# Transposing the rows' maxima: TensorE's transpose against VectorE's 32 by 32 blocks

## The chip, the cores and the metric

The kernel runs on one core of one Trainium2 chip. A core has TensorE (PE in the profile, with its weight loads as PEld), VectorE (DVE), ScalarE (ACT), GpSimd (POOL) and SyncE (SP), which here only issues DMAs. The metric is the device time of one execution in microseconds, lower is better. Three executions of the kernel before took 850.92, 851.16 and 852.25 us; the median is 851.16 us.

## The reference

The input x has 2048 rows of 640 numbers. It is normalized, xn = layernorm(x), and goes through two branches whose results are multiplied:

```python
xn = _layernorm(x, axis=-1)
s = _A_ref(xn, A_wqkv, A_wo)                         # attention: 32 heads of 20, window of 256 keys
g = _silu(_B_ref(xn, B_w1, B_b1, B_w2, B_b2))        # MLP 640 -> 1536 -> 640, squared relu
return x + s * g
```

In the attention, `scores = q k^T * 20 ** -0.5`, a query sees itself and the 255 keys before it, and a softmax over these keys weighs the values. Everything is float32. The softmax subtracts the largest score of each row before it takes the exponential; how that maximum gets to where it is needed is what the change is about.

## The kernel before, in words

Products are made of split operands: a float32 number is written as a high part that TensorE takes at full speed and a remainder, and three products stand for one.

**First stage** (lines 134 to 406). x is loaded, normalized, transposed and split; the values v and the first columns of q and k are made. q and k go to HBM in split form.

**Second stage, the long one** (lines 1222 to 1267). The 32 heads are worked on as 16 pairs, each pair in 16 steps of 128 queries: 256 steps, and 11 more for what lags behind. The two heads of a pair lie in the two halves of the 128 partitions, so TensorE runs two lanes side by side, lane 0 on partitions 0 to 63 and lane 1 on 64 to 127. A step s does this for its pair p and tile q:

- `scores` (L479): the scores of 128 queries against up to 384 keys, one product in each lane, into the tiles sps (two banks, tag "s").
- `maxima` (L487): VectorE adds the mask and takes each row's maximum, two instructions and two reads of the accumulator, into a column of mt. mt has 128 partitions (the queries) and a column for each head and each of four steps. There are two such tiles, used in turn.
- `scores_t` (L519), nine steps later (LAG): the same scores again, transposed, with keys on the partitions and queries along the free axis. The operands have two rows more: the queries' tile qs carries minus the maximum (high part and remainder) and the keys' tile ks carries ones, so the product comes out with the maximum subtracted.
- `exps` (L525 to L528): ScalarE takes the exponential out of the one pair tile stps, GpSimd cuts off what is masked.
- `values` (L547), once in four steps, two steps later again: probabilities times values.

Every four steps the columns of mt must become rows of qs. That is `max_rows` (L489 to L505), called in the step after the fourth (s % 4 == 0, L1250). TensorE transposes mt with an identity, 64 by 64 in each lane (L494), into an unused part of that step's stps. ScalarE copies eight rows out with the sign turned (L500, tile row), copies them again as high part (L501, tile mrow), GpSimd makes the remainder (L502), and two DMAs write them into qs (L504).

**What fills the time between.** All engines' orders are written out by hand (`manual_schedule`): what the program emits first, an engine does first. A generator, `filler`, hands out the remaining matrix products (the rest of q and k as qkps, the MLP's two layers as hps and yps, all L469) half a product per lane at a time. A planner keeps one clock per lane; each emitted product adds a fixed cost from a table (`COST`, L42: 0.067 for 128 columns, 0.12 for 256, 0.147 for 320). In each step `fill` emits filler until lane 0's clock reaches the step's share, `pace` times the step's number. `pace` (L1200) is the sum of the filler and of the scores and values, without the transposes of the maxima, divided by the steps. The transposes add COST[128] = 0.067 to each lane (`both`, L495). A filler product needs one of three PSUM banks, which comes free when VectorE (L888 for qkps, L996 for yps) or ScalarE (L961 for hps) has read it out: the eviction.

**Third stage, the output** (`out_filler`, L1150). When the filler is used up, the attention's result, loaded back from HBM (ob, L1107, and the sums' inverses, L1108), is scaled by VectorE (L1123), split (L1124, L1127) and multiplied by wo (wops, L607), and the result is multiplied by silu of the MLP, added to x and stored. It may begin while the last steps still run: the filler goes over into it.

Of the kernel before, what the change touches and what calls it, by code (L numbers as in the profile page):

```python
# [29 lines left out]
HP = P // 2  # L30
HALF = D // 2
# [22 lines left out]
def f32(ap):  # L54
    return ap.bitcast(F32)
# [3 lines left out]
def attn_mlp_kernel(ctx: ExitStack, tc, x, wqkv, wo, w1, b1, w2, b2, out):  # L59
# [38 lines left out]
    mts = [const.tile([P, HP], F32, name=f"mt{j}") for j in range(2)]  # L98
# [22 lines left out]
    def ones_rows(i):  # L121
        for h in range(2):
            nc.sync.dma_start(f32(ks[i])[h * HP + KR:h * HP + KR + 2].rearrange("a (c n) -> a c n", n=P), ones.unsqueeze(1).to_broadcast([2, S // P, P]))

# [9 lines left out]
    with tc.tile_pool(name="ph1v", bufs=2) as p1v, tc.tile_pool(name="ph1", bufs=2) as p1, tc.tile_pool(name="ph1x", bufs=4) as p1b, tc.tile_pool(name="ph1w", bufs=1) as p1w, tc.tile_pool(name="ph1t", bufs=2, space=PSUM) as p1t:  # L134
# [129 lines left out]
        with tc.manual_schedule(engines={E_.PE, E_.Activation, E_.DVE, E_.Pool, E_.SP}):  # L264
# [99 lines left out]
            for b in range(NB):  # L364
# [8 lines left out]
                if b == 0:  # L373
# [8 lines left out]
                    def loads1():  # L382
                        load_x(2)
                        spill_x(0)
                        nc.sync.dma_start(b1t, b1.rearrange("(c p) -> p c", p=P))
                        nc.sync.dma_start(b2t, b2.partition_broadcast(P))
                        ones_rows(0)
                        raws.extend(load_w(group_src(1, w), KC) for w in "qk")
# [100 lines left out]
    def max_rows(p, g, tps):  # L489
        i = p % 2  # L490

        def one(j):
            r = slice(j * HP, (j + 1) * HP)
            nc.tensor.transpose(tps[:HP, j, 3 * P:3 * P + HP], mts[g % 2][r, :], ident[r, r])  # L494
        both(lambda: one(0), lambda: one(1), COST[P])  # L495

        def rest():
            row = at2.tile([8, P], F32, tag="row", bufs=1, name="row")
            mrow = at2.tile([8, 2, P], F32R, tag="mrow", bufs=1, name="mrow")
            nc.scalar.activation(row.rearrange("m (j n) -> m j n", j=2), tps[:8, :, 3 * P:3 * P + HP], AF.Copy, scale=-1.0)  # L500
            nc.scalar.activation(mrow[:, 0, :], row, AF.Copy)  # L501
            nc.gpsimd.tensor_sub(mrow[:, 1, :], row, f32(mrow[:, 0, :]))  # L502
# [6 lines left out]
    def pair_tile():  # L509
        return ptp.tile([P, 2, BT], F32, tag="st", name="stps")  # L510
# [703 lines left out]
    with tc.manual_schedule(engines={E_.PE, E_.Activation, E_.DVE, E_.Pool, E_.SP}):  # L1214
        load_v(0)
        nc.vector.memset(ot, 0.0)
        loads = []
# [4 lines left out]
        for s in range(steps):  # L1222
# [8 lines left out]
            if a:  # L1231
# [3 lines left out]
                if s == 2:  # L1235
                    ones_rows(1)
# [8 lines left out]
            rows = None  # L1245
# [53 lines left out]
```

## Time and profile before

| | before |
|---|---|
| median of three executions | 851.16 us (850.92 to 852.25) |
| span of the profiled execution, first to last instruction | 849.5 us |
| TensorE's mean granted clock in it | 0.999 |
| TensorE busy / VectorE / ScalarE / GpSimd | 841.8 / 457.9 / 420.9 / 330.4 us |
| the long stage, first to last L479 | 116.7 to 739.4 us |
| products of the output, L607 | 774.2 to 845 us |

The profiled execution has no time of its own beside its span; its span of 849.5 us is 1.7 us less than the median. In rows of groups the columns are line, engine, operation, tiles and shapes and count, then busy us and mean ns of one, then idle time of the engine just before them with what ended it. In rows of time the first number is the start, the second the duration, both in us. In rows by windows each engine's busy time stands with the number of its instructions, then the granted clock, the share of time that the 16 DMA engines were busy, and GB/s. "PE busy" counts a time as busy when either lane works.

### The profile page before, as it was taken

What the parts mean: (1) busy time and instruction counts of PE and PEld (TensorE: products, weight loads), DVE (VectorE), ACT (ScalarE), POOL (GpSimd) and SP (SyncE); (2) the same over time, 40 slices, a digit from 0 to 9 for tenths busy, and PEclk for the clock granted to TensorE, in tenths of its full rate; (3) what the DMA queues carried; (4) which work ended last, traced back from release to release, by engine and by line L of the source; (5) the groups of instructions that cost most, each with busy time, mean ns of one, the idle gap of its engine ahead of it and who ended that gap; (6) DMA issues with size and microseconds to landing.
All of it is one profiled execution on the core that took longest, in us unless ns stands there. A gap on an engine that the chain in (4) does not pass through costs nothing.

```text
span 849.5 us, 25542 instructions
## 1 busy us (share of the span) xinstructions
PE 841.8 (99%) x10160; PEld 784.3 (92%) x10160; DVE 457.9 (54%) x1370; ACT 420.9 (50%) x792; POOL 330.4 (39%) x652
## 2 busy tenths in 40 slices
PE   9999999999999999999999999999999999999997
PEld 8999999888888999999999999999999999999997
DVE  7653126665567645455445466755455455436753
ACT  5232114545556763664653664853763754763321
POOL 6010002434334553553552553643553543542442
PEclk9999999999999999999999999999999999999999
DMA  7997587868979565337248245576456355467993
GB/s 248 316 403 286 176 207 260 268 215 266 309 246 288 152 196 151 93 116 200 79 151 219 86 126 151 141 224 188 111 163 199 109 166 190 129 155 212 291 233 118
DMA packets 94398, 166.42 MB, mean 196 GB/s; under 512 B 10952, under 2 KB 43848, under 8 KB 93256
## 3 DMA queue, kind: packets, MB, share of 16 engines
q1 hardware_dynamic: 94120, 164.64, 63.9%
q8 instruction: 80, 1.31, 0.7%
q14 instruction: 38, 0.31, 0.1%
q10 hardware_dynamic: 160, 0.16, 0.1%
HBM read 93.66 MB, written 70.52 MB: 193 GB/s over the span
## 4 chain that ended last, share of the span: by engine, by line
PE 97%; DVE 1%; DMA 1%; issue 0%; ACT 0%; SPq 0%; DVEq 0%
PE yps L469 21%; PE hps L469 21%; PE qkps L469 14%; PE ops L547 10%; PE wops L607 8%; PE vps L229 8%; PE stps L519 5%; PE sps L479 4%; PE qkps L206 3%; PE tps L173 1%; DMA qs<-q_d 0%; DMA xt<-in_A_x_dram 0%; PE tps L302 0%; PE stps L494 0%; PE warm_ps L316 0%
## 5 line engine op out<-in xcount | busy, mean ns | idle before, releaser
L487 DVE CUSTOM_DVE_ANT_0 junk<-sps,mask 128x384 bf16<-128x384 f32 (+2 forms) x512 | 272.6, 532 | 257.7 <-PE hps L469 73.4
L525 ACT ACTIVATE p<-stps 128x768 f32<-128x768 f32 (+2 forms) x256 | 197.4, 771 | 257.2 <-PE stps L519 209.8
L526 POOL TENSOR_SCALAR_AFFINE_SELECT p<-p 128x256 f32<-128x256 f32 x256 | 110.1, 430 | 322.3 <-ACT p L525 317.0
L469 PE MATMUL yps<-w,hh 64*128 64x320 f32 x1536 | 228.3, 310 | 0.8 <-DVE ysb L996 0.7
L469 PE MATMUL hps<-xb,w 64*128 64x256 f32 (+1 forms) x2100 | 218.6, 305 | 0.0
L469 PEld LDWEIGHTS hps<-xb,w 64*128 64x128 f32 x2100 | 199.2, 187 | 6.2 <-issue 5.1
L469 PEld LDWEIGHTS yps<-w,hh 64*128 64x128 f32 x1536 | 181.9, 185 | 5.9 <-issue 3.4
L469 PE MATMUL yps<-w,hl 64*128 64x320 f32 x768 | 174.1, 309 | 0.0
L479 PE MATMUL sps<-ks,qs 60*128 60x384 f32 (+2 forms) x512 | 142.5, 340 | 0.2 <-DVE mt L487 0.2
L519 PE MATMUL stps<-qs,ks 62*128 62x384 f32 (+2 forms) x512 | 136.0, 330 | 0.1
L469 PEld LDWEIGHTS yps<-w,hl 64*128 64x128 f32 x768 | 113.7, 185 | 1.7 <-issue 1.7
L469 PE MATMUL qkps<-xT,wgkh 64*128 64x512 f32 x320 | 100.4, 395 | 0.0
L469 PE MATMUL qkps<-xT,wgqh 64*128 64x512 f32 x320 | 97.8, 392 | 0.0
L528 POOL TENSOR_SCALAR_AFFINE_SELECT p<-p 128x256 f32<-128x256 f32 x224 | 93.6, 418 | 0.0
L547 PE MATMUL ops<-p,vp 128*21 128x128 f32 (+1 forms) x2112 | 92.8, 313 | 0.0
L519 PEld LDWEIGHTS stps<-qs,ks 62*128 62x128 f32 x512 | 88.2, 187 | 1.3 <-issue 0.4
L479 PEld LDWEIGHTS sps<-ks,qs 60*128 60x128 f32 x512 | 86.2, 185 | 2.3 <-DVE mt L487 0.8
L547 PEld LDWEIGHTS ops<-p,vp 128*21 128x21 f32 x2112 | 65.2, 100 | 23.6 <-issue 11.6
L229 PE MATMUL vps<-wv,xT 128*128 128x320 f32 x480 | 71.5, 308 | 0.0
L229 PEld LDWEIGHTS vps<-wv,xT 128*128 128x128 f32 x480 | 70.5, 188 | 0.1
L966 POOL TENSOR_TENSOR hl<-sq,hh 128x512 fp32r<-128x512 f32 x48 | 62.2, 1297 | 18.9 <-ACT sq L965 18.8
L607 PE MATMUL wops<-wo,oT 128*128 128x320 f32 x384 | 61.6, 309 | 0.0
(104 smaller groups left out, 1165.0 us busy)
## 6 DMA issues: line engine op xcount, KB each, us to landing
ks<-k_d SPq DMA_DIRECT2D x64, 240.0 KB
qs<-q_d SPq DMA_DIRECT2D x64, 240.0 KB
xb<-xs SPq DMA_DIRECT2D x60, 256.0 KB
xs<-xT SPq DMA_DIRECT2D x8, 1280.0 KB
k_d<-shm SPq DMA_DIRECT2D x19, 512.0 KB
q_d<-shm SPq DMA_DIRECT2D x19, 512.0 KB
y<-ysb SPq DMA_DIRECT2D x28, 320.0 KB
o<-osb SPq DMA_DIRECT2D x64, 128.0 KB
```

What stands on the lines that cost most here:

```text
L206: nc.tensor.matmul(ps, wt[:, c, :], xT[part][b][:, c * BT + t0:c * BT + t0 + n], start=m == 1, stop=m == 3 * KC)
L229: nc.tensor.matmul(ps, xT[xp][b][:, c * BT + t * P: c * BT + (t + 1) * P], wv[wp][:, c, nh * HALF:(nh + 1) * HALF], start=first and m == 0 ...
L469: return nc.tensor.matmul(out, a[r], b_[r], skip_group_check=True, **kw)
L479: nc.tensor.matmul(ss[hh][:, :nk], qs[i][o, q * P:(q + 1) * P], ks[i][o, k0 * P:k0 * P + nk], start=True, stop=True)
L487: nc.vector.tensor_tensor_reduce(out=junk[:, :nk], in0=ss[hh][:, :nk], in1=mask[:, 3 * P - nk:], scale=1.0, scalar=-3.0e38, op0=ALU.add, o ...
L519: nc.tensor.matmul(tps[:, hh, :n], ks[i][o, kb * P:(kb + 1) * P], qs[i][o, kb * P:kb * P + n], start=True, stop=True)
L525: nc.scalar.activation(p32[:, :, :n], tps[:, :, :n], AF.Exp, scale=SCALE)
L526: nc.gpsimd.affine_select(p32[:, :, 0:P], p32[:, :, 0:P], pattern=[[0, 2], [1, P]], compare_op=ALU.is_ge, fill=0.0, base=0, channel_multip ...
L528: nc.gpsimd.affine_select(p32[:, :, 2 * P:], p32[:, :, 2 * P:], pattern=[[0, 2], [-1, P]], compare_op=ALU.is_gt, fill=0.0, base=0, channel ...
L547: nc.tensor.matmul(ot[r0:r0 + VW, c0:c0 + len(part), :], vps[p][:, kb // 4, kb % 4, hh, :], pt[:, hh, :].rearrange("p (t n) -> p t n", n=P ...
L607: nc.tensor.matmul(ps, a, b_, start=j == 0, stop=j == n - 1)
L966: nc.gpsimd.tensor_sub(hh[1][:, :BT], sq, f32(hh[0]))
```

## The change

- The four steps' maxima are no longer transposed by TensorE. VectorE does it with four instructions, each a transpose of a block of 32 by 32 of mt into a strip of row, which is now a tile in SBUF of 32 rows. They are emitted right after the fourth step's maxima (s % 4 == 3) and not in the next step; the rest of `max_rows` still runs in the next step, after the exponentials.
- The transposes no longer add their 0.067 to the planner's clocks, and no longer write into stps.
- ScalarE's copy with the turned sign (L500) is gone. The rows of keys hold minus one instead of one, and qs gets the maxima with their own sign.
- mt has 32 columns instead of 64.

```diff
-    ones = const.tile([2, P], F32, name="ones")
-    nc.gpsimd.memset(ones, 1.0)
+    minus = const.tile([2, P], F32, name="minus")
+    nc.gpsimd.memset(minus, -1.0)
...
-    def max_rows(p, g, tps):
+    def max_rows(p, g):
         i = p % 2
-
-        def one(j):
-            r = slice(j * HP, (j + 1) * HP)
-            nc.tensor.transpose(tps[:HP, j, 3 * P:3 * P + HP], mts[g % 2][r, :], ident[r, r])
-        both(lambda: one(0), lambda: one(1), COST[P])
+        row = at2.tile([SQ, P], F32, tag="row", bufs=1, name="row")
+        for r in range(0, P, SQ):
+            nc.vector.transpose(row[:, r:r + SQ], mts[g % 2][r:r + SQ, :])
 
         def rest():
-            row = at2.tile([8, P], F32, tag="row", bufs=1, name="row")
             mrow = at2.tile([8, 2, P], F32R, tag="mrow", bufs=1, name="mrow")
-            nc.scalar.activation(row.rearrange("m (j n) -> m j n", j=2), tps[:8, :, 3 * P:3 * P + HP], AF.Copy, scale=-1.0)
-            nc.scalar.activation(mrow[:, 0, :], row, AF.Copy)
-            nc.gpsimd.tensor_sub(mrow[:, 1, :], row, f32(mrow[:, 0, :]))
+            nc.scalar.activation(mrow[:, 0, :], row[:8], AF.Copy)
+            nc.gpsimd.tensor_sub(mrow[:, 1, :], row[:8], f32(mrow[:, 0, :]))
...
-            rows = None
+            rows, made = made, None
...
-            if s % 4 == 0 and 0 < s <= NP * NT:
-                rows = max_rows((s - 1) // NT, (s - 1) % NT // 4, stp[0] if b else pair_tile())
             if a:
                 maxima(*a, *sc)
+                if a[1] % 4 == 3:
+                    made = max_rows(p, q // 4)
```

Where instructions move is seen in the engines' orders. VectorE in the changed program, around one group of four steps (junk and mt are the maxima, here L488; L993 is the eviction that was L996):

```order
L488 ISA junk,mt_100<-sps,mask 128x384
L488 ISA mt_100 128x1
L494 STREAM_TRANSPOSE row<-mt_100 32x32 x4
L993 TENSOR_TENSOR ysb<-yps,b2t 128x320
L488 ISA junk,mt_101<-sps,mask 128x384
```

The four transposes stand between the last maxima of a group and whatever followed them; here it is the eviction of a filler bank, as directly behind 14 of the 64 groups.

TensorE before, in a step with s % 4 == 0 (sps and stps are the scores and the transposed scores, yps is filler):

```order
L479 MATMUL sps<-ks_117,qs_116 128x128 x2
L519 MATMUL stps<-qs_1350,ks_1351 128x384 x2
L494 MATMUL stps<-ident,mt_101 64x64 x2
L469 MATMUL yps<-w_0_0_3886,hl 128x320 x2
L469 MATMUL yps<-w_0_0_3886,hh 128x320 x2
```

In the changed program (its L516 makes the transposed scores, its L470 the filler) the same step has the filler directly behind the transposed scores:

```order
L480 MATMUL sps<-ks_117,qs_116 128x128 x2
L516 MATMUL stps<-qs_1350,ks_1351 128x384 x2
L470 MATMUL yps<-w_0_2_4007,hh 128x320
L470 MATMUL yps<-w_0_0_3785,hh 128x320
L470 MATMUL yps<-w_0_0_3785,hl 128x320
```

The pair of transposes is gone, and since the planner's clocks lack its cost, filler moves up. Where that ends is seen on TensorE at the end of the attention. Before, the last values (L547) are followed by filler, 52 half products of it, and only then by the output:

```order
L547 MATMUL ops<-p_13921,vp_12681 21x256 x2
L547 MATMUL ops<-p_13921,vp_12681 21x128 x2
L547 MATMUL ops<-p_13962,vp_12681 21x128 x4
L547 MATMUL ops<-p_14006,vp_12681 21x128 x2
L469 MATMUL yps<-w_1_1_9330,hh 128x320
L469 MATMUL yps<-w_1_2_9481,hh 128x320
```

In the changed program (its L604 is the output's wops, its L544 the values) the filler is used up sooner, and 18 products of the output come ahead of the last values:

```order
L604 MATMUL wops<-wo_13790,oT_14079 128x320
L544 MATMUL ops<-p_14008,vp_12804 21x256 x2
L544 MATMUL ops<-p_14008,vp_12804 21x128 x2
...
L544 MATMUL ops<-p_14152,vp_12804 21x128 x2
L604 MATMUL wops<-wo_13790,oT_14079 128x320
```

So the output's first products now come between the last scores and the last values of the attention.

More of the change, by code (lines that the diff above doesn't have):

```diff
@@ L97, in attn_mlp_kernel @@
     nc.gpsimd.affine_select(mask[:, 2 * P:], mask[:, 2 * P:], pattern=[[-1, P]], compare_op=ALU.is_ge, fill=NEG, base=0, channel_multiplier=1)
[L98 removed]
+    mts = [const.tile([P, SQ], F32, name=f"mt{j}") for j in range(2)]
     for t_ in mts:
         nc.gpsimd.memset(t_, 0.0)
[L101 to L102 removed]
+    minus = const.tile([2, P], F32, name="minus")
+    nc.gpsimd.memset(minus, -1.0)
     eps = const.tile([P, 1], F32, name="eps")
@@ L1216, in attn_mlp_kernel @@
         nc.vector.memset(ot, 0.0)
-        loads = []
+        loads, made = [], None
         def at_step(n):
```

9 lines of the change are left out of this document (5 added, 4 removed).

## The prediction

> **What bounds the kernel now.** I read the page's first part, then the chain of work that ended last, then the windows of the long stage.
>
> ```profile
> span 849.5 us, 25542 instructions
> PE 841.8 (99%) x10160; PEld 784.3 (92%) x10160; DVE 457.9 (54%) x1370; ACT 420.9 (50%) x792; POOL 330.4 (39%) x652
> PE 97%; DVE 1%; DMA 1%; issue 0%; ACT 0%; SPq 0%; DVEq 0%
> 117.00:740.00 623.00, 622.00 (x8452) 571.44 (x8451) 346.77 (x1163) 350.02 (x663) 271.06 (x570) 1.00 0.60 181
> ```
>
> TensorE sets the end: it is busy for 99% of the span and is 97% of the chain. In the window of the long stage (columns PE, PEld, DVE, ACT, POOL) it is busy for 622.0 of 623.0 us, and VectorE for 346.8. So a lane's time that TensorE no longer needs is time won, as long as nobody else makes TensorE wait. But "busy" holds when one of the two lanes works, so what an instruction costs a lane must be read from starts. TensorE's rows in order of time, around one transpose of the maxima:
>
> ```profile
> 398.77 0.28 PE L469 MATMUL hps<-xb,w 64*128 64x256 f32 x1
> 398.82 0.31 PE L469 MATMUL yps<-w,hh 64*128 64x320 f32 x1
> 398.89 0.28 PE L469 MATMUL hps<-xb,w 64*128 64x256 f32 x1
> 398.97 0.31 PE L469 MATMUL yps<-w,hh 64*128 64x320 f32 x1
> ...
> 399.97 0.22 PE L494 MATMUL stps<-ident,mt 64*64 64x64 f32 x1
> 400.00 0.36 PE L469 MATMUL hps<-xb,w 64*128 64x256 f32 x1
> 400.03 0.34 PE L519 MATMUL stps<-qs,ks 62*128 62x384 f32 x1
> 400.20 0.28 PE L469 MATMUL hps<-xb,w 64*128 64x256 f32 x1
> 400.21 0.22 PE L494 MATMUL stps<-ident,mt 64*64 64x64 f32 x1
> 400.24 0.39 PE L469 MATMUL yps<-w,hh 64*128 64x320 f32 x1
> 400.32 0.39 PE L469 MATMUL hps<-xb,w 64*128 64x256 f32 x2
> 400.47 0.30 PE L469 MATMUL yps<-w,hl 64*128 64x320 f32 x1
> ```
>
> At this place lane 0 works on hps and lane 1 on yps. Undisturbed, an hps follows an hps after 0.12 us (398.77, 398.89) and a yps a yps after 0.15 us (398.82, 398.97). With the transpose: lane 0 starts it at 399.97, an hps at 400.00 and the next at 400.20. The transpose and one hps take 0.23 us, so the transpose costs 0.23 - 0.12 = 0.11 us. Lane 1: 400.21, then a yps at 400.24 and the next at 400.47, so 0.26 - 0.15 = 0.11 us. The product behind the transpose starts 0.03 us after it, but its record is 0.08 us longer than its like (0.36 against 0.28, 0.39 against 0.31).
>
> **The change, part by part.**
>
> *The transposes leave TensorE.* Their group:
>
> ```profile
> L494 PE MATMUL stps<-ident,mt x128: 216/217/219, 126.7 to 741.7; 64*64 64x64 f32 x128
> ```
>
> 128 transposes are 64 pairs, the two of a pair in two lanes side by side: 64 x 0.11 = 7.0 us. The bounds are 64 x 0.03 = 1.9 us, if only the distance of starts counted, and 64 x 0.217 = 13.9 us, if a record's whole length did. I take 7.0, since two lanes with different products agree on it.
>
> [...]
>
> The planner charged 0.067 for a pair. Now it hands out 0.067 of filler more in these steps: 64 x 0.067 = 4.3 us of the 7.0 come out of the end of the filler, and the other 2.7 us out of the steps, which get shorter by what the planner had not counted.
>
> *VectorE gets 256 instructions.* The trace has no transpose on VectorE. Its nearest rows are small instructions and the smallest full one:
>
> ```profile
> L487 DVE DVE_READ_ACCUMULATOR2_ANT mt<- 128x1 f32 x512 | 42.4, 83 | 0.0
> L799 DVE TENSOR_TENSOR w<-raw,w 128x128 fp32r<-128x128 f32 x4 | 1.1, 286 | 0.0
> L296 DVE RECIPROCAL rstd<-rstd 128x1 f32<-128x1 f32 x4 | 0.6, 143 | 0.0
> ```
>
> The transposes also wait for VectorE's own read of the accumulator, as each maximum waits for the one before. VectorE's rows in time, in a place where an eviction stands behind a group:
>
> ```profile
> 437.37 0.09 DVE L487 DVE_READ_ACCUMULATOR2_ANT mt<- 128x1 f32 x1
> 437.60 0.56 DVE L487 CUSTOM_DVE_ANT_0 junk<-sps,mask 128x384 bf16<-128x384 f32 x1
> 438.09 0.08 DVE L487 DVE_READ_ACCUMULATOR2_ANT mt<- 128x1 f32 x1
> 438.09 0.49 DVE L996 TENSOR_TENSOR ysb<-yps,b2t 128x320 f32<-128x320 f32 x1
> 439.42 0.56 DVE L487 CUSTOM_DVE_ANT_0 junk<-sps,mask 128x384 bf16<-128x384 f32 x1 [0.84 <-PE sps L479]
> ```
>
> That wait is 437.60 - 437.46 = 0.14 us. A group then costs between 0.14 + 4 x 0.083 = 0.47 us and 0.14 + 4 x 0.286 = 1.28 us. I take 0.14 + 4 x 0.12 = 0.62 us, between the accumulator's read and the reciprocal, because a block has 32 columns and little but fixed cost. That is 64 x 0.62 = 40 us on an engine that has 623 - 347 = 276 us free in this stage.
>
> [...]
>
> Who waits for VectorE? The next maxima do not suffer: in the rows above VectorE stands idle for 0.84 us before them, which covers 0.62. What suffers is an eviction directly behind a group, because the filler's next product needs its bank:
>
> ```profile
> L469 PE MATMUL yps<-w,hl x768: 299/306/413, 301.3 to 773.9; 64*128 64x320 f32 x192
>   PE yps L469: 16.8, 20
>   DVE ysb L996: 1.9, 3
> ```
>
> These are the waits on the tile yps: evictions waited 20 times for TensorE, so often they have time; TensorE stood visibly behind an eviction only 3 times, 1.9 us in all, but shorter waits vanish in "busy". 14 of the 64 groups have an eviction directly behind them in the changed order. I take four of these as spots where the bank is wanted at once, and 0.5 us for each (0.62 less one product of a lane, 0.12, already on its way): 2.0 us lost. The ends are 0 and 14 x 1.28 = 17.9 us.
>
> *ScalarE loses a copy, the DMAs stay.*
>
> ```profile
> L500 ACT ACTIVATE row<-stps x64: 244/249/268, 127.1 to 742.7; 8x128 f32<-8x128 f32 x64
>   PEld stps L519: 0.3, 1
> ```
>
> ScalarE has 64 x 0.249 = 16 us less. TensorE waited for this copy once, 0.3 us, so it is worth 0 to 0.3 us; the cover is the three steps between the rows' making (step 4g + 4) and their first use (step 4g + 7). The two DMAs of each group, the keys' rows (same size, another constant) and GpSimd's remainder stay as they are. If the rows came late, scores_t would wait; they come earlier.
>
> *The end moves up.* 4.3 us of filler no longer lie behind the last values. In the windows (columns as before; the last two are DMA share and GB/s):
>
> ```profile
> 764.00:774.00 10.00, 9.91 (x118) 9.13 (x115) 4.35 (x7) 4.56 (x6) 0.00 (x0) 1.00 0.66 167
> 774.00:828.00 54.00, 54.00 (x369) 53.82 (x368) 37.68 (x51) 16.41 (x24) 23.74 (x24) 1.00 0.97 259
> ```
>
> While the output's products run, the DMA engines are busy for 0.97 of the time, and TensorE still does not wait. Just before they have a third free, so their work can begin earlier along with the products. I take 0; the ends are 0 and the whole 4.3 us.
>
> Sum: -7.0 + 2.0 = -5.0 us. The span becomes 849.5 - 5.0 = 844.5. With the 1.7 us between span and median, which I leave as they are, the forecast is **846.2 us**.
>
> **The rivals.**
>
> *A, the DMAs of the output bind.* For it: the 0.97 above. Against it: TensorE busy for 54.00 of 54.00. If the loads do not come earlier, TensorE waits in the output for the 4.3 us that left the filler: -5.0 + 4.3 = -0.7, 850.5 us.
>
> *B, VectorE becomes the bound, slower than before.* Place: the evictions directly behind a group, in the steps with s % 4 == 3. If a group costs 1.28 us and the planner has a bank wanted at most of these 14 spots, each costs 1.2 us or so. From six spots on (7.0 / 1.2 = 5.8) the change loses; with ten it is -7.0 + 12.0 = +5.0, 856.2 us. For it: in VectorE's rows above the eviction follows the last maximum at the very moment that it ends, at 438.09, so any delay in front goes into it whole. Against it: VectorE is free for 44% of the stage, and evictions waited for TensorE 20 times.
>
> *C, the lanes were idle anyway.* If what a lane loses to a transpose is given back by another wait, only the distance of starts counts, 1.9 us, against 2.0 lost: +0.1, 851.3 us. For it: "busy" cannot show a lane that stands. Against it: the 0.11 us in both lanes.
>
> **How the numbers follow.** Forecast 0.70 with its own range of 843.5 to 848.5, from a little more than the full 7.0 us with no spot at all to eight spots at 0.5 or four at 1.2; A 0.12, C 0.08, B 0.10. A measurement of this kernel can tell 0.2%, 1.7 us, from no change. Faster by more than that: the forecast's 0.70 and the larger part of A with part of the loss only, 0.09, so 0.79. Within it: the rest of A and most of C, 0.11. Slower: B, 0.10. The range is 842.5 to 850.8: it holds the forecast's own range, 1 us beyond it below, and A; B and C, 0.18, are left out.
>
> **What would show it.** Right: TensorE has 128 instructions fewer, and the rows in time show no product with a record 0.08 us longer behind the transposed scores; first to last L479's successor takes some 3 us less than 622.7, and the output starts 7 us or more before 774.2. VectorE's transposes come at 83 to 180 ns each, with busy time near 490 us; the next maxima start as they did after scores; TensorE's waits for the successor of L996 grow by about 2 us. Wrong: evictions that start late behind transposes with TensorE's sequencer standing for more than 7 us in all (B); gaps between the output's products ended by loads of ob or sums (A); steps as long as before (C).

## The result and the profile after

The changed kernel takes 874.65 us (median of 871.81 to 875.14), the kernel before beside it 851.51 us: slower, by a ratio of 1.0265 with an interval of 1.0249 to 1.028. The forecast was 846.2 us with a range to 850.8.

The page of the changed kernel, its first part and the chain that ended last:

```profile
span 873.4 us, 25408 instructions
PE 845.4 (97%) x10032; PEld 783.7 (90%) x10032; DVE 509.3 (58%) x1626; ACT 406.5 (47%) x728; POOL 328.8 (38%) x652
PE 89%; DMA 4%; DVE 4%; issue 1%; SPq 1%; ACT 0%; POOL 0%; DVEq 0%; ACTq 0%
```

TensorE has its 128 instructions fewer, and still it is busy for longer (845.4 against 841.8 us) in a span that is 23.9 us longer. Its share of the chain fell from 97% to 89%; DMA and VectorE have 4% each. So there are two things to find: waits that stand in the profile, and why TensorE is busy for longer with less to do.

The long stage in one window (TensorE, its weight loads, VectorE, ScalarE, GpSimd; clock; DMA):

```profile
117.00:749.00 632.00, 626.19 (x8387) 571.98 (x8387) 395.91 (x1414) 338.04 (x603) 268.33 (x571) 1.00 0.60 178
```

From the first scores to the last (116.4 to 748.9 us) it takes 632.4 us, before 622.7. It was to be 2.7 us shorter. VectorE has 395.9 us of work there instead of 346.8; in the mean it is still far from full. The mean length of the steps with s % 4 == 0, those behind the transposes, went from 2.474 to 2.608 us; the others changed by 0.03 us or less.

VectorE's transposes, as a group and (second fence) in time:

```profile
L494 DVE STREAM_TRANSPOSE row<-mt x256: 199/200/206, 125.5 to 751.1; 32x32 f32<-32x32 f32 x128
```

```profile
707.66 0.56 DVE L488 CUSTOM_DVE_ANT_0 junk<-sps,mask 128x384 bf16<-128x384 f32 x1
708.14 0.08 DVE L488 DVE_READ_ACCUMULATOR2_ANT mt<- 128x1 f32 x1
708.33 0.84 DVE L494 STREAM_TRANSPOSE row<-mt 32x32 f32<-32x32 f32 x4
```

One takes 0.200 us, four in a row 0.84, and they begin 0.11 us after the accumulator's read ends (708.22): 0.95 us for a group, where 0.62 was taken. 0.84 us is more than four times 0.200, so nothing of the four overlaps.

TensorE's waits over the whole changed kernel (us in total, times, longest):

```profile
PE wops L604 <- DVE res L1184: 9.2, 1, 9.2
PE stps L516 <- ACT p L522: 6.3, 1, 6.3
PE stps L516 <- DMA qs<-mrow: 1.7, 1, 1.7
PE sps L480 <- DVE mt L488: 1.3, 3, 0.8
PE yps L470 <- DVE ysb L993: 1.3, 2, 1.0
```

Two single waits, 15.5 us, lie at the end. Before, TensorE had no visible wait behind 700 us at all.

### The profile page after: what moved, and what is told of

Its sections match the earlier page's. It is cut to its first block, busy times and chain, and to the rows that moved or that the text cites. A ratio compares the mean times of both kernels' runs of the same rounds, so it can differ in the third digit from the quotient of the medians.

```text
span 873.4 us, 25408 instructions
## 1 busy us (share of the span) xinstructions
PE 845.4 (97%) x10032; PEld 783.7 (90%) x10032; DVE 509.3 (58%) x1626; ACT 406.5 (47%) x728; POOL 328.8 (38%) x652
## 4 chain that ended last, share of the span: by engine, by line
PE 89%; DMA 4%; DVE 4%; issue 1%; SPq 1%; ACT 0%; POOL 0%; DVEq 0%; ACTq 0%
PE hps L470 19%; PE yps L470 19%; PE qkps L470 13%; PE ops L544 9%; PE vps L230 8%; PE wops L604 7%; PE stps L516 5%; PE sps L480 4%; PE qkps L207 3%; DVE junk L488 1%; DMA o<-osb 1%; DVE w L796 1%; PE tps L174 1%; DMA qs<-mrow 1%; DMA xb<-xs 1%
## 5 line engine op out<-in xcount | busy, mean ns | idle before, releaser
L488 DVE CUSTOM_DVE_ANT_0 junk<-sps,mask 128x384 bf16<-128x384 f32 (+2 forms) x512 | 272.1, 531 | 221.2 <-PE sps L480 73.4
L522 ACT ACTIVATE p<-stps 128x768 f32<-128x768 f32 (+2 forms) x256 | 197.4, 771 | 276.9 <-PE stps L516 264.0
L523 POOL TENSOR_SCALAR_AFFINE_SELECT p<-p 128x256 f32<-128x256 f32 x256 | 108.5, 424 | 346.8 <-ACT p L522 337.0
L470 PE MATMUL yps<-w,hh 64*128 64x320 f32 x1536 | 230.8, 312 | 2.2 <-DVE ysb L993 1.3
L470 PE MATMUL hps<-xb,w 64*128 64x256 f32 (+1 forms) x2100 | 214.2, 303 | 0.6 <-DVE ysb L993 0.6
L470 PEld LDWEIGHTS hps<-xb,w 64*128 64x128 f32 x2100 | 198.7, 187 | 6.6 <-issue 4.7
L470 PEld LDWEIGHTS yps<-w,hh 64*128 64x128 f32 x1536 | 183.9, 187 | 9.2 <-DVE ysb L993 4.8
L470 PE MATMUL yps<-w,hl 64*128 64x320 f32 x768 | 173.4, 311 | 0.0
L480 PE MATMUL sps<-ks,qs 60*128 60x384 f32 (+2 forms) x512 | 140.1, 342 | 1.5 <-DVE mt L488 1.3
L516 PE MATMUL stps<-qs,ks 62*128 62x384 f32 (+2 forms) x512 | 133.3, 332 | 8.1 <-ACT p L522 6.3
L470 PEld LDWEIGHTS yps<-w,hl 64*128 64x128 f32 x768 | 114.2, 188 | 1.9 <-issue 1.9
L470 PE MATMUL qkps<-xT,wgqh 64*128 64x512 f32 x320 | 99.2, 390 | 0.0
L470 PE MATMUL qkps<-xT,wgkh 64*128 64x512 f32 x320 | 97.5, 391 | 0.0
L525 POOL TENSOR_SCALAR_AFFINE_SELECT p<-p 128x256 f32<-128x256 f32 x224 | 93.9, 419 | 0.0
L516 PEld LDWEIGHTS stps<-qs,ks 62*128 62x128 f32 x512 | 85.8, 188 | 8.9 <-ACT p L522 6.6
L544 PE MATMUL ops<-p,vp 128*21 128x128 f32 (+1 forms) x2112 | 92.8, 313 | 0.0
L480 PEld LDWEIGHTS sps<-ks,qs 60*128 60x128 f32 x512 | 83.3, 185 | 5.5 <-DVE mt L488 4.1
L544 PEld LDWEIGHTS ops<-p,vp 128*21 128x21 f32 x2112 | 65.2, 100 | 23.9 <-issue 12.1
L604 PE MATMUL wops<-wo,oT 128*128 128x320 f32 x384 | 63.5, 315 | 9.2 <-DVE res L1184 9.2
L963 POOL TENSOR_TENSOR hl<-sq,hh 128x512 fp32r<-128x512 f32 x48 | 62.3, 1298 | 16.9 <-ACT sq L962 16.8
```

The costliest lines, as they stand in the source:

```text
L470: return nc.tensor.matmul(out, a[r], b_[r], skip_group_check=True, **kw)
L480: nc.tensor.matmul(ss[hh][:, :nk], qs[i][o, q * P:(q + 1) * P], ks[i][o, k0 * P:k0 * P + nk], start=True, stop=True)
L488: nc.vector.tensor_tensor_reduce(out=junk[:, :nk], in0=ss[hh][:, :nk], in1=mask[:, 3 * P - nk:], scale=1.0, scalar=-3.0e38, op0=ALU.add, o ...
L516: nc.tensor.matmul(tps[:, hh, :n], ks[i][o, kb * P:(kb + 1) * P], qs[i][o, kb * P:kb * P + n], start=True, stop=True)
L522: nc.scalar.activation(p32[:, :, :n], tps[:, :, :n], AF.Exp, scale=SCALE)
L523: nc.gpsimd.affine_select(p32[:, :, 0:P], p32[:, :, 0:P], pattern=[[0, 2], [1, P]], compare_op=ALU.is_ge, fill=0.0, base=0, channel_multip ...
```

## The experiments

Medians below are compared with 851.02 to 851.32 us of the kernel before, timed beside each set.

### Which part of the change costs what

The changed kernel with one line put back, so that TensorE's order is that of before without the transposes (e1_cost_kept):

```diff
+            if s % 4 == 0 and 0 < s <= NP * NT:
+                both(lambda: None, lambda: None, COST[P])
             if a:
                 maxima(*a, *sc)
```

> The changed kernel, but the planner still adds 0.067 to both lanes' clocks in the steps with s % 4 == 0, so TensorE's order is that of the kernel before with the transposes taken out. Theory (two separate losses: the order at the end, where the output starts before the attention has ended, and VectorE's transposes of 0.2 us in the long stage): the two waits of 6.3 and 9.2 us at the end vanish, the long stage stays as long as in the changed kernel or nearly (about 630 us from first to last scores), so about 851.5 - 7.0 + 12 = 856 us, 853 to 860. Rival 1 (VectorE's transposes make the end late too, whatever the order): the waits at the end stay, 868 us or more. Rival 2 (the order makes all the loss, VectorE none): 844 to 847 us.

The kernel before with four transposes of VectorE added, whose result nobody reads (e2_both):

```diff
             if a:
                 maxima(*a, *sc)
+                if a[1] % 4 == 3:
+                    extra = at2.tile([32, P], F32, tag="extra", bufs=1, name="extra")
+                    for r in range(0, P, 32):
+                        nc.vector.transpose(extra[:, r:r + 32], mts[q // 4 % 2][r:r + 32, 0:32])
```

> The kernel before, whole, with four more transposes of 32 by 32 on VectorE after each fourth maxima, whose result nobody reads; TensorE's order is that of before. Theory: what VectorE's transposes cost by themselves, about +12 us, 863 us (859 to 867), all of it in the long stage. Rival 1: +23 us or more, with waits at the end. Rival 2: within 2 us of 851.5.

e1_cost_kept without any transposition; norow is a tile of zeros (e3_neither):

```diff
-        row = at2.tile([SQ, P], F32, tag="row", bufs=1, name="row")
-        for r in range(0, P, SQ):
-            nc.vector.transpose(row[:, r:r + SQ], mts[g % 2][r:r + SQ, :])
+        row = norow
```

> No transposes on any engine; the rows of maxima are zeros, so the softmax subtracts nothing. The planner's cost is kept, so TensorE's order is that of before without the transposes. What the 64 pairs cost TensorE: by the reading of the rows 64 x 0.11 = 7.0 us, 844.5 us (843 to 846). If only the distance of starts counts, 849.6 us. If a record's whole length does, 837.6 us.

The kernel before, transposes on TensorE, but without their cost in the planner, so in the order of the changed kernel (e4_before_nocost):

```diff
-        both(lambda: one(0), lambda: one(1), COST[P])
+        both(lambda: one(0), lambda: one(1), 0.0)
```

> The kernel before with TensorE's transposes, but the planner counts nothing for them, so that TensorE's order is that of the changed kernel plus the transposes; VectorE has no transposes. Theory: the end's two waits come from the order alone: about 851.5 + 15 to 19 = 867 to 871 us, with the two waits of several us each at the same products. Rival 1 (VectorE does it): 850 to 853 us.

Later one more was added: e1_cost_kept with its transposes in place, but rows of zeros behind them (e14_behind_unread):

```diff
-            nc.scalar.activation(mrow[:, 0, :], row[:8], AF.Copy)
-            nc.gpsimd.tensor_sub(mrow[:, 1, :], row[:8], f32(mrow[:, 0, :]))
+            nc.scalar.activation(mrow[:, 0, :], norow[:8], AF.Copy)
+            nc.gpsimd.tensor_sub(mrow[:, 1, :], norow[:8], f32(mrow[:, 0, :]))
```

> The same cut where the four transposes stand directly behind the maxima (857.84 us with the planner's cost kept): VectorE's time stays, the rows are zeros, so the exponentials subtract no maxima. Theory 1 (the whole 13.8 us above 844.05 are VectorE's time): 857 to 859 us. Theory 2 (10.9 us are VectorE's time, as in the kernel before with four unread transposes, 2.9 us the rows' chain): 854 to 856 us.

| kernel | median us | against before, ratio and interval |
|---|---|---|
| e3_neither | 844.05 | 0.992 [0.9904, 0.9937] |
| e14_behind_unread | 855.26 | 1.005 [1.0035, 1.0065] |
| e1_cost_kept | 857.84 | 1.0081 [1.0066, 1.0096] |
| e2_both | 861.97 | 1.013 [1.0115, 1.0145] |
| e4_before_nocost | 870.38 | 1.0223 [1.0208, 1.0239] |
| changed kernel | 874.65 | 1.0265 [1.0249, 1.028] |

The steps between them are the account of the change: 851.05 - 844.05 = 7.0 us won (TensorE's transposes, ScalarE's copy and the rows' wait for them together), where the prediction has 64 x 0.11 = 7.0 for the transposes alone; +11.2 for VectorE's time, whoever reads the result (10.9 by e2_both); some +2.6 for the rows that now wait for VectorE (a rough size: e1_cost_kept ran from 856.77 to 859.28 us, e14_behind_unread from 854.81 to 857.01); +16.8 for the planner's missing cost. The last is the largest, and e4_before_nocost has it with no VectorE transpose in the kernel at all: 19.3 us for taking 0.067 off a number. Its TensorE stands at the same two places as in the changed kernel (its L607, L1187, L519 and L525 are L604, L1184, L516 and L522 there), and e1_cost_kept shows no wait of TensorE behind 700 us:

```profile
PE wops L607 <- DVE res L1187: 9.3, 1, 9.3
PE stps L519 <- ACT p L525: 5.2, 1, 5.2
```

### Behind the maxima: who is delayed

VectorE in e1_cost_kept, in a place where the eviction L993 stands behind the group, and TensorE's first matmul after it:

```profile
438.79 0.08 DVE L488 DVE_READ_ACCUMULATOR2_ANT mt<- 128x1 f32 x1
438.98 0.84 DVE L494 STREAM_TRANSPOSE row<-mt 32x32 f32<-32x32 f32 x4
439.85 0.49 DVE L993 TENSOR_TENSOR ysb<-yps,b2t 128x320 f32<-128x320 f32 x1
441.16 0.56 DVE L488 CUSTOM_DVE_ANT_0 junk<-sps,mask 128x384 bf16<-128x384 f32 x1 [0.82 <-PE sps L480]
```

```profile
439.18 0.31 PE L470 MATMUL yps<-w,hh 64*128 64x320 f32 x1
440.39 0.55 PE L470 MATMUL yps<-w,hh 64*128 64x320 f32 x3 [0.91 <-DVE ysb L993]
```

The eviction would have begun with the accumulator's read, at 438.79, as it did before at 438.09; it begins 1.06 us later, and TensorE stands for 0.91 us of that. Right behind, VectorE itself stands idle for 0.82 us: the engine has time, the bank behind it has not.

Three edits move the time away from there. Half of each group behind the next maxima (e5_split; `second` is `blocks(HP)`, called behind the next step's maxima):

```diff
+        def blocks(r0):
+            for r in range(r0, r0 + HP, SQ):
+                nc.vector.transpose(row[:, r:r + SQ], mts[g % 2][r:r + SQ, :])
+        blocks(0)
...
+            if second:
+                second()
```

> The changed kernel with the planner's cost kept (857.84 us), in which each group of four VectorE transposes is cut in two: two directly after the maxima of step 4g + 3, two after those of step 4g + 4; the copy and the DMAs of the rows follow behind the second half, one step later than ScalarE's copy had them. Theory 1 (only what reaches beyond VectorE's idle time in a step, 0.7 to 1.4 us, costs anything, so that two halves of 0.42 us cost less than half of one group of 0.84 us): 846 to 851 us. Theory 2 (VectorE's time costs the same wherever it stands in a step, 13.8 us of 857.84 for 64 groups): 855 to 859 us.

The whole group at the head of the next step, behind the evictions (e6_after_evictions):

```diff
+                rows = max_rows((s - 1) // NT, (s - 1) % NT // 4)
             if a:
                 maxima(*a, *sc)
-                if a[1] % 4 == 3:
-                    made = max_rows(p, q // 4)
```

> The changed kernel with the planner's cost kept (857.84 us), in which the four VectorE transposes of a group stand at the head of the next step: behind the evictions of step 4g + 3, ahead of the maxima of step 4g + 4. Theory 1 (the loss is the evictions that stand directly behind the group and TensorE's banks of the filler that wait for them): 845 to 851 us. Theory 2 (the loss is the next pair of maxima, which now begins up to 0.84 us later, and the bank of the scores that it frees): 855 to 860 us. If both carry it, a time between.

One instruction for the four blocks, gathered by ScalarE (e7_one_instruction):

```diff
-        for r in range(0, P, SQ):
-            nc.vector.transpose(row[:, r:r + SQ], mts[g % 2][r:r + SQ, :])
+        turned = at2.tile([P, SQ], F32, tag="turned", bufs=1, name="turned")
+        nc.vector.transpose(turned, mts[g % 2])
         def rest():
+            for r in range(0, P, SQ):
+                nc.scalar.activation(row[:8, r:r + SQ], turned[r:r + 8, :], AF.Copy)
```

> The changed kernel with the planner's cost kept (857.84 us), in which one VectorE instruction transposes the four blocks of a group (128 x 32 into 128 x 32) in place of four of 32 x 32, and ScalarE gathers the four blocks' first 8 rows with four small copies, behind the exponentials of the next step, ahead of the copy that was there. Theory 1 (the loss is VectorE's time behind the maxima, 0.84 us a group; the one instruction takes 0.2 to 0.3 us and ScalarE has room for four copies of some 0.2 us in every fourth step): 844.5 to 849 us. Theory 2 (the loss comes from a further wait on VectorE in the order of the step, not from its time): 854 to 858 us. If ScalarE's four copies delay the next exponentials, over 850 us with waits of TensorE for p.

And the kernel before with two unread transposes instead of four (e8_two; in the edit of e2_both the loop ends at HP):

> The kernel before with two unused VectorE transposes of 32 x 32 behind the maxima of each step 4g + 3 in place of the four that gave 861.97 us (10.9 us over before). Theory 1 (what VectorE's idle time takes in is free, the loss grows faster than the time): 852 to 854.5 us. Theory 2 (the loss is in proportion to VectorE's time): 856 to 857.5 us.

e5_split: 859.45 us, no better than 857.84 and just above the range of its second theory; but its rows are also a step later (TensorE waits 2.6 us for them), and ScalarE's copy of them stands ahead of that step's exponentials, so it tells little by itself. e6_after_evictions: 848.83 us, 9.0 us won, and faster than before (0.9974 [0.9964, 0.9985]). e7_one_instruction: 850.66, 7.2 us won, but above the range of its first theory; ScalarE's copies come up below. e8_two: 855.15, between its theories: 4.1 us for half the time that costs 10.9, so the loss grows faster than the time, though not from a sharp point on. TensorE's waits for the eviction in e1_cost_kept and, second, in e6_after_evictions:

```profile
PE yps L470 <- DVE ysb L993: 4.3, 6, 1.6
PE hps L470 <- DVE ysb L993: 1.7, 2, 0.9
```

```profile
PE yps L470 <- DVE ysb L993: 1.0, 2, 0.8
```

The waits behind the eviction fall from 6.0 to 1.0 us. TensorE's busy time falls with it, from 842.4 to 838.3 us, with the same instructions. That would be lanes that stand while the other works, which count as busy as with the 0.11 us of a transpose; in e1_cost_kept a stretch at half clock comes on top (last section). How the rest of the 9.0 us divides between the two was not measured.

### What is left at the head of the next step

Both remedies together (e9_one_after), and e6_after_evictions with rows of zeros, by the edit of e14_behind_unread (e13_after_unread):

```diff
-                if a[1] % 4 == 3:
-                    made = max_rows(p, q // 4)
...
+        nc.vector.transpose(turned, mts[g % 2])
```

> Both remedies at once, with the planner's cost kept: one VectorE instruction of 128 x 32 (212 ns) in place of four (0.84 us), standing at the head of the next step, behind the evictions of step 4g + 3. Theory (two separate losses: evictions behind the group 9.0 us of 857.84, and VectorE's time ahead of the next maxima, 4.8 us in 848.83, which shrinks with it from 0.84 to 0.21 us): 844.5 to 847.5 us. Rival (what is left above the 844.05 us without any transposition is the rows' chain that ends later, or ScalarE's four extra copies, not VectorE's time): 848 to 850 us.

> The four VectorE transposes at the head of the next step (848.83 us), but their result is not read: ScalarE's copy and GpSimd's difference take rows of zeros instead, so the exponentials subtract no maxima. VectorE's time stays, the wait of the rows' chain for VectorE is gone. Theory 1 (the 4.8 us above 844.05 are VectorE's time ahead of the next maxima): 848 to 849 us. Theory 2 (they are the rows' chain that waits for VectorE): 844 to 845 us.

e9_one_after came to 848.34 us (0.9963 [0.9949, 0.9977]), hardly better than 848.83, although VectorE's time fell to a quarter; that was its rival. e13_after_unread: 848.59, so the 4.5 us above e3_neither are VectorE's time there, not the rows' chain. The two agree only if something in e9 took VectorE's gain back. The tile turned in e9_one_after's like, e7_one_instruction:

```profile
L498 ACT ACTIVATE row<-turned x256: 208/227/231, 125.9 to 742.3; 8x32 f32<-8x32 f32 x128
L494 DVE STREAM_TRANSPOSE turned<-mt x64: 211/212/215, 125.6 to 740.0; 128x32 f32<-128x32 f32 x64
```

ScalarE has four copies of 0.227 us more in each group. Two kernels leave these copies out and take rows of zeros, at the head (e17_one_after_unread) and behind the maxima (e18_one_behind_unread); below, what they leave out of e9_one_after and e7_one_instruction:

> One VectorE instruction of 128 x 32 (0.21 us) at the head of the next step, its result not gathered and not read: no ScalarE copies of blocks, rows of zeros, so the exponentials subtract no maxima. Theory 1 (the price follows VectorE's time, a quarter of 4.5 us; ScalarE's four copies made up the rest of 848.34 us): 844.5 to 846 us. Theory 2 (the price sets in with the first instruction, whatever its length): 847.5 to 849 us.

> The same directly behind the maxima, ahead of the evictions. Theory 1 (the price follows VectorE's time, a quarter of 11.2 us): 846 to 847.5 us. Theory 2 (the price grows faster than the time, so that 0.21 us cost next to nothing): 844 to 845.5 us. Theory 3 (it sets in with the first instruction): 849 us or more.

```diff
-            for r in range(0, P, SQ):
-                nc.scalar.activation(row[:8, r:r + SQ], turned[r:r + 8, :], AF.Copy)
```

They take 844.00 and 845.86 us, the first as its first theory said, the second just under it. ScalarE's copies, with the rows' wait for VectorE, cost 848.34 - 844.00 = 4.3 us, and 850.66 - 845.86 = 4.8 us in the other place; at the head the rows' wait is at most 0.2 us of it (848.83 - 848.59). Whom the copies delay was not taken apart. Of TensorE's waits, e9_one_after has 0.8 us for ScalarE's eviction of hps that e17_one_after_unread does not have. VectorE's time against what it costs, above the 844.05 of e3_neither:

| VectorE's time in a group | behind the maxima | at the head of the next step |
|---|---|---|
| 0.21 us | 1.8 us (e18) | 0.0 us (e17) |
| 0.84 us | 11.2 us (e14) | 4.5 us (e13) |

Four times the time costs six times as much behind the maxima, and from nothing to 4.5 us at the head. (The number of instructions, one and four, changes along with the time.) So idle time in front of the maxima does cover 0.21 us, but not 0.84. The traces say why: in the kernel before, VectorE stands idle in front of the first maxima of the step behind a group for 0.81 us in the median, but for less than 0.84 us in 38 of 63 places, and for less than 0.21 us in only 6. In e13_after_unread these maxima begin 0.44 us after the end of their scores in the mean, in e17_one_after_unread 0.22 us and in e3_neither 0.21 us.

GpSimd as the gatherer instead of ScalarE (e15_pool_gathers, here against e9_one_after):

```diff
-                nc.scalar.activation(row[:8, r:r + SQ], turned[r:r + 8, :], AF.Copy)
+                nc.gpsimd.tensor_copy(row[:8, r:r + SQ], turned[r:r + 8, :])
```

> One VectorE instruction of 128 x 32 at the head of the next step, its four blocks gathered by GpSimd instead of ScalarE (848.34 us). Theory 1 (ScalarE's four copies of 227 ns, 0.9 us a group, are what holds that kernel 4.3 us above 844.05): 845 to 847 us. Theory 2 (they are hidden; the rest is something else): 848 to 850 us, or more where GpSimd's copies delay its masks of the exponentials.

873.75 us, 25 us worse than with ScalarE. Only the last clause of the second theory, a delay through GpSimd's masks, left room for so much. Waits of ScalarE and of TensorE in it:

```profile
ACT mrow L500 <- POOL row L498: 96.5, 54, 2.5
PE stps L518 <- ACT p L524: 8.1, 13, 1.5
```

ScalarE's copy to mrow now waits for GpSimd 54 times, and GpSimd's copies stand in order behind its masks of the exponentials that ScalarE has just made: ScalarE, GpSimd, ScalarE in a row, with the next exponentials queued behind. TensorE waits 13 times for exponentials, 8.1 us, where e17_one_after_unread has no such wait; the rest of the 25 us is not visible as one wait.

### The end

Names in what follows: osb is the result of a group of heads' queries before its store, rec the inverses of the sums, ob the result loaded back, oT its split form, res the rows of the output.

ScalarE, VectorE and SyncE in the changed kernel, where TensorE waits for p (until 777.6) and for res (until 807.7); a fence for each engine:

```profile
766.74 0.81 ACT L522 ACTIVATE p<-stps 128x768 f32<-128x768 f32 x1 [1.09 <-PE stps L516]
775.39 0.63 ACT L1121 ACTIVATE oT<-ob 128x512 fp32r<-128x512 f32 x1 [7.84 <-DVE ob L1120]
...
777.01 0.58 ACT L522 ACTIVATE p<-stps 128x512 f32<-128x512 f32 x1
...
790.01 0.39 ACT L549 ACTIVATE osb<-ops 128x256 f32<-128x256 f32 x1
```

```profile
774.66 1.56 DVE L1120 TENSOR_TENSOR ob<-ob,sums 128x512 f32<-128x512 f32 x2 [8.12 <-DMA ob<-o]
...
790.24 0.94 DVE L1063 RECIPROCAL rec<-rec 128x128 f32<-128x128 f32 x1
805.93 0.95 DVE L1063 RECIPROCAL rec<-rec 128x128 f32<-128x128 f32 x1 [14.74 <-DMA rec<-o]
806.80 1.22 DVE L1184 TENSOR_TENSOR res<-wops,yq 128x320 f32<-128x320 f32 x3
```

```profile
765.97 1.98 SPq L1104 DMA_DIRECT2D ob<-o  x4
...
789.37 2.26 SPq L1093 DMA_DIRECT2D xres<-in_A_x_dram  x5
791.67 0.91 SPq L1082 DMA_DIRECT2D yq<-y  x2
792.62 2.66 SPq L1104 DMA_DIRECT2D ob<-o  x4
796.15 0.56 SPq L1105 DMA_DIRECT2D sums<-rec  x1
797.15 0.34 SPq L569 DMA_DIRECT2D o<-osb  x1
798.46 0.34 SPq L1064 DMA_DIRECT2D rec<-rec  x1
803.03 1.19 SPq L1061 DMA_DIRECT2D rec<-o  x2
```

First wait: the load of ob is issued from 765.97 on and has landed by 774.66. ScalarE's copy oT stands in its order ahead of an exponential and waits 7.84 us; the exponential's pair tile is the only one, so TensorE stands. Second wait: VectorE stands 14.74 us at the last group's reciprocal, whose load is issued at 803.03, behind the store of that group's result at 797.15. Three evictions of the output (806.80, x3) stand behind it in order. The store itself is late because of a third order, SyncE's: ScalarE has the group's result ready at 790.40, but the store is issued 6.75 us later, behind nine further loads for the output. In the kernel before, the same store was issued 3.0 us after its result (768.42, 771.43), behind five loads. There the load of the reciprocal was issued 6.15 us behind the store, here 5.9, so that part did not change. In the kernel before the same reciprocal waits a ninth as long:

```profile
781.22 0.95 DVE L1066 RECIPROCAL rec<-rec 128x128 f32<-128x128 f32 x1 [1.61 <-DMA rec<-o]
```

The order of TensorE's rows tells what changed: the output's first product stood 53 rows behind the last values, now 18 products of the output stand ahead of the last group of values in the trace, so the output runs on groups whose transfers have not been made.

Three kernels take away the orders on ScalarE and VectorE, not SyncE's and not the transfers. The turning of the first output tile behind the last exponentials (e10_turn_later), the last two reciprocals four output groups later (e11_recip_later), and both (e12_both_later):

```diff
-            if j >= 6:
-                turn_out(0, 0)
             if j >= 7:
-                turn_out(0, 1)
+                turn_out(0, 0)
                 load(2)
```

```diff
+            elif recs[g] is not None and over and waits.setdefault(g, 4) > 0:
+                waits[g] -= 1
             elif recs[g] is not None and (state[2] >= stored(g) + 6 if not over else True):
                 nc.vector.reciprocal(recs[g], recs[g])
```

> The changed kernel (874.65 us, the planner's cost gone) with one edit at the end: ScalarE's and VectorE's turning of the first output tile (the scaling of ob, the copy to oT) is not placed ahead of the last exponentials but behind them, with the output itself. Theory 1 (the wait of 6.3 us of TensorE for p at 777.6 is ScalarE standing in order behind a copy whose loads had not landed; each of the two large waits is a loss of its own): 866 to 869.5 us. Theory 2 (the loads of the end are late whatever waits for them, so the wait only moves to the output's first matmuls or into the second wait): 873 to 876 us.

> The changed kernel (874.65 us) with one edit at the end: VectorE's reciprocals of the last two groups stand four output groups later in its order, behind evictions of the output that they had stood ahead of. Theory 1 (the wait of 9.2 us of TensorE at 807.7 is VectorE standing in order at a reciprocal whose load had not landed): 863 to 868 us, since with it go the reduced clock of the stretch behind it. Theory 2 (the chain of the last group, store, load, reciprocal, store, load, is too late for the output anyway, and a later reciprocal makes it later): 873 to 880 us, with TensorE's wait at the matmuls of the last groups.

> Both edits of the end together, in the changed kernel (874.65 us). Theory 1 (two in-order waits, 6.3 and 9.2 us and the reduced clock behind them, are what the planner's missing cost brought): 856 to 861 us, about the 857.84 us that the changed kernel has with the cost kept. Theory 2 (the late transfers bind the end by themselves): 867 us or more.

And e6_after_evictions with half of the planner's cost, which puts the output's first product 31 rows behind the last values (e16_half_cost):

> The four transposes at the head of the next step (848.83 us), the planner's cost of a transposition halved, so that the output's first matmuls stand between the place that they have with the whole cost (53 rows of TensorE behind the last values) and with none (20 rows ahead of them): 31 rows behind. Theory 1 (the end's waits set in only where the output runs into its own loads; ahead of that point the earlier output costs nothing): 847 to 849.5 us. Theory 2 (each matmul that moves forward costs its share of 16.8 us): 855 to 859 us.

| kernel | median us | over its like with the whole cost | TensorE's waits behind 700 us, in its profile |
|---|---|---|---|
| changed kernel | 874.65 | 16.8 | 9.2 res + 6.3 p + 1.7 rows = 17.2 |
| e10_turn_later | 871.80 | 14.0 | 9.7 res + 4.2 oT + 0.7 rows = 14.6 |
| e11_recip_later | 867.21 | 9.4 | 6.8 p + 3.0 res + 1.5 rows = 11.3 |
| e12_both_later | 865.16 | 7.3 | 3.5 oT + 2.4 res + 0.8 rows = 6.7 |
| e16_half_cost | 849.96 | 1.1 | 1.1 yps |

The waits of e12_both_later, whose profiled execution was its fastest, 2.1 us below the median, and VectorE at the first of them:

```profile
PE wops L604 <- DVE oT L1124: 3.5, 1, 3.5
PE wops L604 <- DVE res L1184: 2.4, 1, 2.4
PE stps L516 <- DMA qs<-mrow: 0.8, 1, 0.8
```

```profile
777.96 0.89 DVE L991 TENSOR_TENSOR ysb<-yps,yin 128x320 f32<-128x320 f32 x2 [4.23 <-DMA yin<-y]
778.76 1.55 DVE L1124 TENSOR_TENSOR oT<-ob,oT 128x512 fp32r<-128x512 f32 x2
```

Neither theory held whole. The two orders taken away account for 9.5 of the 16.8 us (874.65 - 865.16); with them gone TensorE still waits 6.7 us, now at the output's products. Other orders are left in that: the split of oT stands on VectorE behind an eviction of the filler that waits 4.23 us for its own load (yin), and on SyncE the last group's store is still issued 6.7 us after its result (785.35, 792.01). No kernel changed these, so how much of the remaining 7.3 us the transfers would cost by themselves stays open. In e10 the wait for p mostly moved on to oT, as its second theory said, and 2.9 us were won. In e11 most of the wait for res went, as its first theory said, 7.4 us. And e16_half_cost shows that the price is not in proportion: half of the planner's cost taken away costs 1.1 us (848.83 to 849.96); the whole costs 16.8, measured with the transposes behind the maxima.

## Why the prediction was wrong

**"64 x 0.11 = 7.0 us": right.** 851.05 - 844.05 = 7.0, with ScalarE's copy in it. Reading the lanes from starts gave the size, the record's 0.217 us would have given 13.9.

**"I take 0.14 + 4 x 0.12 = 0.62 us": too small, inside its bounds.** 0.11 + 0.84 = 0.95 us. One transpose of 32 x 32 took 0.200 us where 0.12 was taken, hardly less than the 0.212 us of one over 128 x 32 (e7_one_instruction).

**"I take four of these as spots where the bank is wanted at once, and 0.5 us for each: 2.0 us": this step failed.** VectorE's time cost 11.2 us. It lay inside the ends that the text gave, 0 and 17.9, so what failed was the choice near the lower one. The row that spoke for the upper one was quoted: the eviction follows the accumulator's read at the very moment (438.09). "Evictions waited 20 times for TensorE, so often they have time" was the wrong inference; it counts waits, not how much room the others have. The row "DVE ysb L996: 1.9, 3" was also misread: it holds two waits of weight loads, and the matmuls stood behind that eviction once, for 0.7 us. Rival B had the mechanism and the place, with ten spots and a chance of 0.10.

**"The next maxima do not suffer: 0.84 us idle covers 0.62": failed too.** One step's idle time was taken for all; in 38 of 63 places it is less, in 13 of them less than 0.62. At the head of the step, where the maxima stand directly behind it, the group costs 4.5 us; 0.21 us there cost nothing. In e1_cost_kept, 33 groups are followed by the next maxima within 0.05 us, so they suffer behind the maxima too.

**The rows "come earlier": not so.** Rows that wait for VectorE behind the maxima cost some 2.6 us (857.84 - 855.26). The worth of ScalarE's copy, "0 to 0.3 us", was not measured by itself.

**"The end moves up. I take 0; the ends are 0 and the whole 4.3 us": this step failed most.** It cost 16.8 us. That 4.3 us of filler would leave the end was right: in e4_before_nocost the long stage takes 626.9 us, 4.2 more than before. The step then asked whether the DMA engines have bandwidth for an earlier output, and for a third of the time they had (a share of 0.66 from 764 to 774 us). It did not ask when each load can be issued, nor what stands behind the waiting instruction on ScalarE, VectorE and SyncE. Free bandwidth did not move the transfer that waits for a store: the last group's load was issued at 803.03, 5.9 us behind the store, and the DMA engines were busy for 0.52 of the us before 802 and for 0.08 of the next. And 4.3 us was no upper end: VectorE's reciprocal waited 14.74 us, and the three evictions behind it in order were held back with it. Rival A looked at the same place: that the loads do not come earlier was right, that the DMA engines' bandwidth would be the reason was not shown, and its end of 4.3 us was the same wrong one.

Without the planner's part the change would still be slower than before, 857.84 us; with the transposes behind the evictions and the cost kept it is faster, 848.83, or 848.34 with one instruction. The forecast's 846.2 needed a VectorE price of 2 us, which behind the maxima only one instruction comes near to, in a kernel that leaves out the gathering copies and the rows (845.86).

## What to carry to other kernels

When an instruction goes into an engine's order, its price is read from what stands directly behind it and how soon that is wanted, not from the engine's idle share: the same 0.84 us cost 11.2 us ahead of an eviction and 4.5 us behind it. A cost in a planner's table also places work; taking it out moves whatever comes last, so look at the last transfers' issue times and at the in-order waits there before it counts as nothing. And a vector transposition of blocks belongs in one instruction over all partitions, if the gathering behind it is cheaper than what it saves: here it took 0.212 us in place of 0.84, and four copies on ScalarE gave 4.3 us back. Where the last transfers matter, read the order of the engine that issues them too: here a finished result waited 6.75 us for its store behind nine loads.

## What the runs showed of the hardware

After a wait TensorE's clock was halved for some 3 us: it was 0.50 in place of 1.00 up to 780.8 behind the wait that ends at 777.6, and up to 811.5 behind the one that ends at 807.7. The changed kernel around the second of these, in windows of 1 us (columns as before, the clock is the first number after the engines), and TensorE's rows there:

```profile
808.60:809.60 1.00, 1.00 (x5) 1.00 (x5) 1.00 (x2) 0.63 (x1) 1.00 (x2) 0.50 0.46 51
811.60:812.60 1.00, 1.00 (x9) 1.00 (x8) 1.00 (x1) 0.80 (x2) 0.69 (x1) 1.00 0.96 333
```

```profile
796.11 1.92 PE L604 MATMUL wops<-wo,oT 128*128 128x320 f32 x12
807.68 3.57 PE L604 MATMUL wops<-wo,oT 128*128 128x320 f32 x12 [9.21 <-DVE res L1184]
```

Twelve matmuls of the same shape took 3.57 us in place of 1.92. Each of the two long waits cost some 1.6 us more in this way (3.57 - 1.92, and half of the 3.2 us from 777.6 to 780.8). That is one part of why TensorE is busy for longer: it is busy for 834.2 us in e3_neither, 842.4 in e1_cost_kept with VectorE's transposes and one such stretch, and 845.4 in the changed kernel with three. A far shorter wait did it too: in e1_cost_kept one of 1.63 us, at 522.1 (TensorE alone, then the clock):

```profile
519.00:520.30 1.30, 1.30 (x18) 1.00 0.58 145
523.10:524.10 1.00, 1.00 (x11) 0.50 1.07 401
```

The clock was 0.50 for 3.41 us there, from 522.4 to 525.8. The wait of 1.73 us for the rows in the changed kernel, at 708.8, did it too (0.50 from 709.1 to 712.5). Single waits of 1.33 us (e14_behind_unread), 1.44 (e5_split), 1.46 (e15_pool_gathers) and 1.54 (e11_recip_later, at 707.5) did not. The length of the wait does not decide alone: in e15_pool_gathers the clock fell at 252.7 behind a wait of 1.09 us, with TensorE busy for 1.64 of the 3 us from 249 to 252.
